# Re-ordering the opening of a transform-then-expert-layer kernel: merged row loads, rows and weight columns on another DMA queue

## The chip, the cores and the metric

The kernel runs on one core of one Trainium2 chip. The metric is the device time of one execution, in microseconds (us). Lower is better. A difference counts as "same" when it is within 2%.

## The reference

```python
def reference(x, moe_w_in, moe_w_out):          # x: 8 x 3008 x 256, float32
    X = np.fft.fft(np.fft.fft(x, axis=1), axis=2).real   # along the rows, then the channels
    h = X.reshape(8 * 3008, 256) @ moe_w_in              # 256 x 2048
    g = h * np.cos(h)
    return g @ moe_w_out                                 # 2048 x 256
```

## The kernel before

The transform along the rows is done with matrices of cosines and sines (`MC`, "the DFT"), and the transform along the channels is multiplied into the weights (`Wc`, `Ws`). Symmetries of the transform let the kernel fold the rows of a batch four to one before it multiplies. After an opening, it repeats one step of about 4.75 us 376 times (DFT work of the next batch comes in between). In a step TensorE (PE) multiplies (`H`, then `pA` to `pD`), ScalarE (ACT) and VectorE (DVE) compute h·cos h, and GpSimd (POOL) makes four sums of blocks (`G<-G`) which TensorE needs. During the steps POOL also folds the rows of the next batch.

All that the change touches happens in the first 120 us. The parts are these.

*Rows of a batch.* Four tiles `xl0` to `xl3` hold one batch. `xl0` and `xl3` are read in row order by direct DMAs, `xl1` and `xl2` against it by gathers on POOL's queue. The last 512 columns of `xl0` and `xl3` come in two halves of 64 partitions.

```python
def spin(**kw):                      # a load on SP's queue, kept in program order
    pin(nc.sync.dma_start(**kw))

def load_x(b, gather=True):
    ...                              # the four gathers, on POOL's queue
    for j, row in ((0, 0), (3, HALF)):
        spin(out=L[j][:, 0 : 4 * ND], in_=xrows(b, row, 4, 128, 4))       # 512 KB
        for h in range(2):                                                # 2 x 128 KB
            spin(
                out=L[j][64 * h : 64 * h + 64, 4 * ND :],
                in_=xrows(b, row + 512 + 2 * h, 4, 64, 2),
            )
```

*Channel 128.* This channel has no mirror image and is treated apart, for all eight batches at once. It is read element by element: four loads of 8 x 768 elements of 4 bytes each ("single-channel loads"), written to a scratch area in DRAM, and read back in another shape as `xs`. POOL folds `xs` in `fold_ext`, which TensorE needs near step 12.

```python
copy(0, 0, 768, 0, 1)                # rows forward and backward, from both ends:
copy(1, 1, 768, SEQ - 1, -1)         # 6144 descriptors of 4 bytes each
copy(2, 0, 768, HALF, -1)
copy(3, 0, 768, HALF, 1)
```

*Weight columns of channel 128.* `fold_sin(q)` computes a quarter of `Ws`, and four small DMAs turn its last row into columns (`wex`).

```python
def fold_sin(q, tag="H"):
    ps = fold_mms(q, 128, tag)
    act(Ws[:, q * 512 : (q + 1) * 512], ps)
    eng = nc.gpsimd if q > 1 else nc.scalar
    for f in range(4):
        c = q * 512 + f * 128
        pin(eng.dma_start(out=wex[q][:, f : f + 1], in_=Ws[127:128, c : c + 128]))
```

*The order of work.* A list of events `at(time, function)`, sorted by a nominal time (T is one step), sets each engine's order. Two entries matter here: the load of batch 1 and POOL's sums of output weights (`sum_weights(i)`, four small operations each, written to `WT`).

```python
for i in range(8):
    at((i - 1) * T + 1.3, lambda i=i: sum_weights(i))
...
l0 = s0 - (8 if b > 1 else 1.5)                          # s0 = 0 for batch 1
at(l0 * T + 0.1, lambda b=b: state.update(L=load_x(b, b == 1)))
```

## Time and profile before

| quantity | value |
|---|---|
| three runs before the prediction | 1984.85, 1979.04, 1977.92 us |
| the profiled execution | 1985.11 us (span of the core 1983.3) |
| TensorE busy | 1941.3 us, 98% |
| share of TensorE in the chain of waits | 92% |

The page of the kernel before begins as follows. The first line is the span, the second gives busy time, share of the span and number of instructions of each engine, the third is the chain that ended last, by engine.

```profile
span 1983.3 us, 28191 instructions
PE 1941.3 (98%) x8863; PEld 1654.7 (83%) x8863; DVE 1416.7 (71%) x2349; ACT 1452.6 (73%) x2791; POOL 1351.8 (68%) x1862
...
PE 92%; DVE 3%; ACT 1%; issue 1%; POOL 1%; DMA 0%; SPq 0%; DVEq 0%; POOLq 0%
```

TensorE is the limit, and the change takes no work from it. Only the 42 us in which it is not busy, and time in which it runs slowly, can be won. The waits of the first 165 us say where they are. The columns are total us, number of waits and the longest one.

```profile
PE pB L265 <- POOL G L274: 23.4, 3, 20.9
...
POOL e L349 <- DMA xl<-in_x_dram: 21.8, 1, 21.8
...
PE pA L265 <- issue: 2.4, 1, 2.4
```

One wait of 20.9 us stands out, and another engine, POOL, waits 21.8 us for rows. The timeline of TensorE in the kernel before shows when. The columns are start, duration, engine, line, operation, tiles and shapes, and in brackets the idle time before it and what ended it.

```profile
22.59 4.40 PE L265 MATMUL H<-w,CC 128*128 128x512 f32 x6 [1.78 <-DMA w<-in_moe_w_in_dram]
26.82 1.45 PE L265 MATMUL pA<-MC,e 128*128 128x189 f32 x8
...
36.40 1.03 PE L265 MATMUL H<-Rr,Wc 128*128 128x256 f32 x4
...
84.03 0.59 PE L265 MATMUL pB<-G,w 128*128 128x256 f32 x2
105.49 1.22 PE L265 MATMUL pB<-G,WT 128*128 128x256 f32 x2 [20.87 <-POOL G L274]
106.51 1.91 PE L265 MATMUL H<-Ir,Ws 127*128 127x256 f32 x4
...
113.10 0.59 PE L265 MATMUL pB<-G,WT 128*128 128x256 f32 x2
```

The first DFT starts at 26.82, step 0 at 36.40 (its first product is `H<-Rr,Wc`). In program order TensorE runs `H` two steps ahead of the products `pA` to `pD`. The first `pA` to `pD`, those of step 0, therefore come after the `H` of step 2, and what is called a wait in step 0 below lies between the starts of steps 2 and 3. From about 84.6 to 105.5 TensorE stands still. The same pair of matmuls takes 1.22 us after the gap and 0.59 us later: it runs at half speed for a while. The timeline of POOL in the kernel before, with the same columns, shows what it waited for.

```profile
76.40 3.02 POOL L274 TENSOR_TENSOR G<-G 128x256 f32<-128x256 f32 x4
101.19 0.20 POOL L349 COPY e<-xl 128x6 f32<-128x6 f32 x1 [21.77 <-DMA xl<-in_x_dram]
101.34 1.93 POOL L328 TENSOR_TENSOR e<-xl 128x381 f32<-128x381 f32 x2
103.24 3.00 POOL L274 TENSOR_TENSOR G<-G 128x256 f32<-128x256 f32 x4
...
129.23 0.40 POOL L274 TENSOR_TENSOR xs<-xs 128x96 f32<-128x96 f32 x1
```

The kernel pins POOL's work in program order (`pin`). Its fold of batch 1 (`e<-xl`) comes before its sums of the next step (`G<-G`), and its rows were late. The timeline of SP's queue in the kernel before tells why; the duration is the time that SP needed to issue a group.

```profile
12.75 5.71 SPq L207 DMA_DIRECT2D w<-in_moe_w_in_dram  x2
...
29.62 48.86 SPq L168 DMA_DIRECT2D x<-in_x_dram  x5
78.60 17.27 SPq L168 DMA_DIRECT2D xl<-in_x_dram  x6
95.91 4.88 SPq L168 DMA_DIRECT2D xe_dr<-x  x4
```

SP's loads are pinned in program order too, and it spent 48.86 us on issuing the single-channel loads (`x<-in_x_dram`, four long ones and a short one) before it could issue batch 1's rows at 78.60. From the completion records in the trace, the four long loads landed at 56.9, 69.4, 83.7 and 98.2 us. That is 12.5 to 14.5 us each.

The windows view of the kernel before gives a stretch and its length, then the busy time (and number of instructions) of PE, PEld (TensorE's weight loads), DVE, ACT and POOL, and then TensorE's mean granted clock, the DMA share and GB/s.

```profile
106.00:112.00 6.00, 6.00 (x17) 4.80 (x16) 1.98 (x3) 1.09 (x2) 5.09 (x8) 0.58 0.58 13
112.00:125.00 13.00, 13.00 (x61) 11.09 (x60) 10.19 (x17) 10.14 (x20) 8.08 (x12) 1.00 0.03 3
```

The half speed is thus the granted clock: 0.58 just after the gap, 1.00 later.

### The profile page before, as it was taken

The numbers are of one execution on the slowest core, as the hardware profiler recorded it, in microseconds if no ns is written. First come the engines' busy times: TensorE is split into PE (matmuls) and PEld (weight loads), VectorE is DVE, ScalarE is ACT, GpSimd is POOL, SyncE is SP. The second block draws the span as 40 slices with busy tenths as digits, with TensorE's granted clock in tenths as the row PEclk, the third lists the DMA queues.
The fourth block names the chain that finished last, engine by engine and source line by source line (L and its number), as shares of the span: only waits on it lengthen the run. The fifth ranks groups of instructions, "written<-read, shape, count | busy, mean of one in ns | idle before, by whom it ended". The sixth has DMA issues, their size and how long they took to land.

```text
span 1983.3 us, 28191 instructions
## 1 busy us (share of the span) xinstructions
PE 1941.3 (98%) x8863; PEld 1654.7 (83%) x8863; DVE 1416.7 (71%) x2349; ACT 1452.6 (73%) x2791; POOL 1351.8 (68%) x1862
## 2 busy tenths in 40 slices
PE   8689999999999999999999999999999999999998
PEld 4568888888888888888888888888888888887887
DVE  4557767777677776777767776777777776677777
ACT  2557777777777777777777777777777777777776
POOL 3578767777587766777667776678667776555664
PEclk9889999999999999999999999999999999999999
DMA  9920220102200021000310003001030110000101
GB/s 264 23 35 20 51 48 15 26 11 53 49 11 20 12 60 45 18 12 14 73 36 12 15 12 85 16 20 25 8 84 11 22 20 15 16 11 12 22 11 23
DMA packets 261506, 66.17 MB, mean 33 GB/s; under 512 B 248499, under 2 KB 251323, under 8 KB 261356
## 3 DMA queue, kind: packets, MB, share of 16 engines
q1 hardware_dynamic: 254188, 51.51, 14.9%
q0 software_dynamic: 3840, 12.59, 2.0%
q8 instruction: 71, 1.16, 0.3%
q14 instruction: 79, 0.65, 0.1%
q10 hardware_dynamic: 3328, 0.27, 0.1%
HBM read 39.48 MB, written 24.79 MB: 32 GB/s over the span
## 4 chain that ended last, share of the span: by engine, by line
PE 92%; DVE 3%; ACT 1%; issue 1%; POOL 1%; DMA 0%; SPq 0%; DVEq 0%; POOLq 0%
PE H L265 36%; PE pB L265 16%; PE pC L265 16%; PE pD L265 16%; PE pA L265 8%; DVE G L719 1%; ACT G L277 1%; DVE v L271 0%; POOL G L274 0%; DMA xl<-in_x_dram 0%; SPq L168 0%; DVE G L271 0%; ACT E L277 0%; DVE M L271 0%; DVE u L271 0%
## 5 line engine op out<-in xcount | busy, mean ns | idle before, releaser
L274 POOL TENSOR_TENSOR G<-G 128x256 f32<-128x256 f32 x1500 | 1076.8, 728 | 565.3 <-DVE G L719 474.1
L719 DVE SCALAR_TENSOR_TENSOR G<-H,G 128x512 f32<-128x512 f32 x376 | 256.9, 683 | 270.4 <-ACT G L277 270.2
L271 DVE TENSOR_TENSOR G<-H,G 128x512 f32<-128x512 f32 x376 | 260.0, 691 | 220.6 <-ACT G L277 217.6
L277 ACT ACTIVATE G<-H 128x512 int32<-128x512 f32 x376 | 224.5, 597 | 256.6 <-DVE G L271 255.2
L265 PE MATMUL pC<-G,WT 128*128 128x256 f32 x1504 | 388.1, 380 | 1.7 <-DVE u L271 1.6
L265 PE MATMUL H<-Ir,Ws 127*128 127x256 f32 x1504 | 388.5, 380 | 0.7 <-ACT E L277 0.7
L265 PE MATMUL H<-Rr,Wc 128*128 128x256 f32 x1504 | 387.1, 380 | 0.8 <-ACT H L277 0.8
L277 ACT ACTIVATE H<-Rb,wex 128x256 f32<-128x256 f32 x752 | 360.1, 479 | 26.1 <-DVE G L719 10.4
L277 ACT ACTIVATE E<-H 128x512 f32<-128x512 f32 x376 | 224.2, 596 | 204.8 <-PE H L265 201.0
L265 PEld LDWEIGHTS H<-Rr,Wc 128*128 128x128 f32 x1504 | 283.7, 190 | 48.6 <-ACT H L277 2.8
L265 PEld LDWEIGHTS pC<-G,WT 128*128 128x128 f32 x1504 | 284.5, 190 | 45.5 <-PE H L265 5.1
L265 PEld LDWEIGHTS H<-Ir,Ws 127*128 127x128 f32 x1504 | 283.0, 190 | 45.3 <-ACT E L277 6.2
L271 DVE TENSOR_TENSOR G<-E,H 128x512 f32<-128x512 f32 x376 | 255.2, 679 | 26.1 <-PE H L265 24.6
L277 ACT ACTIVATE G<-G,halfpi 128x512 f32<-128x512 f32 x376 | 269.5, 717 | 1.5 <-DVE G L271 1.5
L271 DVE TENSOR_TENSOR M<-G,M 128x512 f32<-128x512 f32 x376 | 257.6, 685 | 0.0
L719 DVE SCALAR_TENSOR_TENSOR G<-G,M 128x512 f32<-128x512 f32 x376 | 254.2, 676 | 0.4 <-ACT M L277 0.3
L265 PE MATMUL pB<-G,WT 128*128 128x256 f32 x752 | 227.7, 384 | 23.4 <-POOL G L274 23.4
L277 ACT ACTIVATE M<-M,halfpi 128x512 f32<-128x512 f32 x376 | 246.2, 655 | 0.4 <-DVE M L271 0.3
L265 PE MATMUL pA<-G,w 128*128 128x256 f32 x752 | 223.7, 379 | 2.4 <-issue 2.4
L277 ACT ACTIVATE M<-G 128x512 int32<-128x512 f32 x376 | 224.4, 597 | 0.0
L265 PE MATMUL pD<-G,WT 128*128 128x256 f32 x752 | 224.1, 380 | 0.0
L265 PE MATMUL pD<-G,w 128*128 128x256 f32 x752 | 223.8, 379 | 0.0
(132 smaller groups left out, 1793.4 us busy)
## 6 DMA issues: line engine op xcount, KB each, us to landing
out_dram<-ot SPq DMA_DIRECT2D x496, 32.0 KB
xl<-in_x_dram SPq DMA_DIRECT2D x16, 512.0 KB
xl<-in_x_dram SPq DMA_DIRECT2D x32, 128.0 KB
out_dram<-ot SPq DMA_DIRECT2D x256, 2.0 KB
MC<-dft_mats SPq DMA_DIRECT2D x4, 943.5 KB
Rb<-r SPq DMA_DIRECT2D x10, 376.0 KB
w<-in_moe_w_in_dram SPq DMA_DIRECT2D x4, 512.0 KB
w<-in_moe_w_out_dram SPq DMA_DIRECT2D x1, 2048.0 KB
```

Source lines behind the costliest of these rows:

```text
L265: nc.tensor.matmul(out_, lhsT=lhsT, rhs=rhs, start=start, stop=stop, skip_group_check=True)
L271: pin(nc.vector.tensor_tensor(out=o, in0=a, in1=b, op=op))
L274: pin(nc.gpsimd.tensor_tensor(out=o, in0=a, in1=b, op=op))
L277: pin(nc.scalar.activation(out=o, in_=i, func=func, **kw))
L719: nc.vector.scalar_tensor_tensor(out=o, in0=h, scalar=TWO_PI, in1=c, op0=ALU.mult, op1=ALU.mult)
```

## The change

The intent is to open with fewer transfers, to bring the input weights earlier, and to take batch 1's rows off SP's queue. The core of the diff:

```diff
+        eng = nc.gpsimd if b == 1 else nc.sync
         for j, row in ((0, 0), (3, HALF)):
-            spin(out=L[j][:, 0 : 4 * ND], in_=xrows(b, row, 4, 128, 4))
-            for h in range(2):
-                spin(
-                    out=L[j][64 * h : 64 * h + 64, 4 * ND :],
-                    in_=xrows(b, row + 512 + 2 * h, 4, 64, 2),
+            pin(eng.dma_start(out=L[j][:, 0 : 4 * ND], in_=xrows(b, row, 4, 128, 4)))
+            pin(
+                eng.dma_start(
+                    out=L[j][:, 4 * ND :],
+                    in_=bass.AP(
+                        tensor=xt,
+                        offset=x.offset + (b * SEQ + row + 512) * ND,
+                        ap=[[2 * ND, 2], [4 * ND, 64], [1, 2 * ND]],
+                    ),
                 )
+            )
 ...                                   # loads of CC, w_in, MC, w_out, pick: dma_start -> spin
-        eng = nc.gpsimd if q > 1 else nc.scalar
         for f in range(4):
-            pin(eng.dma_start(out=wex[q][:, f : f + 1], in_=Ws[127:128, c : c + 128]))
+            pin(nc.gpsimd.dma_start(out=wex[q][:, f : f + 1], in_=Ws[127:128, c : c + 128]))
 ...
-    warm(8)
+    warm(3)
 ...
-        (T + 3.2, lambda: I_odd.second("pA")),
+        (T + 3.2, lambda: I_odd.second("pC")),
 ...
-    at(e0 + 3 * T + 1.35, lambda: ext_rows(0, gtt))
+    at(e0 + 5 * T + 1.0, lambda: ext_rows(0, vtt))
 ...
-        l0 = s0 - (8 if b > 1 else 1.5)
+        l0 = s0 - (8 if b > 1 else 0.5)
```

In the smaller lines, `warm(n)` issues n matmuls on zeros, `I_odd.second` is one part of a DFT, which moves from bank pA to pC, and `ext_rows(0)` are small sums for channel 128, which move from POOL (`gtt`) to VectorE (`vtt`). `spin` in place of `dma_start` fixes the place of a load in SP's order.

The second half of `w_in` already stood ahead of the DFT matrices on SP in the kernel before. What can move it in time is that fewer transfers stand ahead of it and that ScalarE's column copies no longer share SP's completion semaphores (in the trace of the kernel before they used six of SP's eight).

The merged transfer covers the 128 partitions in two blocks of 64 with a source whose outermost dimension has size 2.

## The prediction

> **What bounds it now.** TensorE is busy 1941 of 1983 us (page, part 1) and the chain of waits is 92% TensorE, so past about 160 us only TensorE work would help, and the change removes none there. What can be won lies before that.
>
> Three losses, all in the opening:
> 1. *Batch 1's rows.* In the timeline TensorE stops from about 84.6 to 105.5 us (20.9 us, waiting for POOL's sums). POOL stands behind the fold of batch 1, which waited 21.8 us for its rows. They sat on the SP queue behind four single-channel loads of 4-byte elements (24,576 descriptors, about 13.5 us each, landing at 56.9, 69.4, 83.7, 98.2 us), and could be issued only at 78.6 to 95.9. After the stop, matmuls run at half rate for 6 us, costing 3.0 more. Together 23.9 us.
> 2. *Start.* TensorE's DFTs begin at 26.8 us. The second half of w_in lands at 22.5, because SP issued it at 12.75 and 18.13: SP and ACT share eight completion semaphores, and SP waited for older transfers and for ACT's small weight-column copies. Rows for the other fold (xl3) land at 17.6.
> 3. TensorE waits 2.35 us at 52.7 for bank pA; the move of I_odd to pC removes that.
>
> **What the change does.** Batch 1 leaves SP: its rows go on POOL's queue after the gathers, by about 50 us, needed near 80 to 85. I expect loss 1 removed completely. The program's order shows ten opening transfers issued without a wait, which alone would be worth about 5 us.
>
> But the merged transfer has a source whose slowest dimension is 2. The Trainium skill, page "DMA: Bandwidth & Descriptors", section "Why a DMA increments its semaphore by 16 and not by 1", says a DMA is spread over the largest k up to 16 dividing both sides' slowest dimensions: here 2 engines in place of 16. This trace agrees for other sizes: 128-row loads leave 16 completion records, 8-row loads 9 (8 and the sequencer's one), 31-row stores 2. A 2-engine merge puts 64 descriptors of 2 KB (108 ns median) on each of two engines, twice; everything behind them on the ring waits for those two. Estimate from these durations: xl0 complete near 19 us (now 12.9), xl3 near 27 (17.6), w_in near 29 (22.5), w_out near 40 (36.5). The start becomes later by about 5 us, not earlier.
>
> **New wait.** POOL's fold_ext needs the single-channel data (loads end, then a DRAM round trip). It ran at 129.2 and had its data at 113. It would now run near 105 to 110[...]: data near 105 (16 engines) to 115 us (2). POOL and then TensorE wait some 2 to 4 us there. Moving ext_rows(0) to DVE gives back 1 to 2 us (TensorE waited 0.6 and 1.9 us at 145 and 152).
>
> **Sum.** -23.9, +5 (start), +2.5 (fold_ext), -1.5: about -18 (1961 us) with two engines; about -27 (1952) if merged transfers spread over 16. I lean to the first: **1959 us**, range **1946 to 1970**. Faster by over 2%: 0.03; within: 0.96; slower: 0.01.
>
> **Right if** in the timeline the gap near 85 to 105 is gone; the merged loads leave 2 or 3 completion records and xl0/xl3 become ready after 17/24 us; DFTs begin after 30; POOL waits for the xs data before fold_ext. **Wrong if** the merged loads leave 16 records, DFTs begin near 22 and the gain is 25 or more; or if batch 1's rows on POOL's queue starve or hold up POOL's own column copies (they wait for the gathers' landing) so that the sums of step 0 come late.

## More of the kernel before

The kernel before varies by itself. In the three sessions with experiments (seven runs each; every session used one chip, and the three used different ones) it took 1972.6 to 1982.2, 1973.1 to 1988.1 and 1973.4 to 1987.0 us.

## The result

| | before | after |
|---|---|---|
| runs, us | 1984.85, 1979.04, 1977.92, 1979.32 | 1973.09, 1973.71, 1973.28, 1977.32 |
| median, us | 1979.18 | 1973.49 |
| ratio (95% interval) | | 0.997 (0.9947 to 0.9993) |

Ratios here and below are the mean time of one kernel's fast runs over that of the other's fast runs of the same rounds, so they are not quite the ratio of the medians quoted. The change gains 5.7 us by the medians, not 20, and lies outside the predicted range of 1946 to 1970. A repetition in another session gave 1973.36 (see `after_again`).

The page of the kernel after:

```profile
span 1971.3 us, 28169 instructions
PE 1940.8 (98%) x8858; PEld 1654.1 (84%) x8858; DVE 1418.2 (72%) x2354; ACT 1452.6 (74%) x2791; POOL 1355.8 (69%) x1869
...
PE 91%; DVE 3%; DMA 2%; ACT 1%; SPq 1%; issue 1%; POOL 1%; DVEq 0%; POOLq 0%
```

TensorE's work is the same, and DMA has appeared in the chain with 2%. The timeline of TensorE in the kernel after:

```profile
28.71 6.01 PE L271 MATMUL H<-w,CC 128*128 128x512 f32 x8 [10.93 <-DMA w<-in_moe_w_in_dram]
34.55 1.45 PE L271 MATMUL pA<-MC,e 128*128 128x189 f32 x8
...
44.13 1.03 PE L271 MATMUL H<-Rr,Wc 128*128 128x256 f32 x4
...
60.65 0.59 PE L271 MATMUL pB<-G,w 128*128 128x256 f32 x2
65.28 1.22 PE L271 MATMUL pB<-G,WT 128*128 128x256 f32 x2 [4.03 <-POOL G L280]
66.29 1.91 PE L271 MATMUL H<-Ir,Ws 127*128 127x256 f32 x4
...
72.92 0.59 PE L271 MATMUL pB<-G,WT 128*128 128x256 f32 x2
```

The gap between 85 and 105 is gone. In its place TensorE waits 10.93 us for the input weights at the start, the DFT begins at 34.55 instead of 26.82, and step 0 at 44.13 instead of 36.40. Then, in the first products of step 0, there is a new wait of 4.03 us for POOL's sums, followed by matmuls at half speed. The windows view of the kernel after, with the same columns as before, shows the granted clock around it:

```profile
65.00:68.00 3.00, 2.72 (x7) 2.19 (x8) 0.00 (x0) 0.00 (x0) 2.84 (x7) 0.50 0.32 56
68.00:71.00 3.00, 3.00 (x9) 2.37 (x8) 1.98 (x3) 1.09 (x2) 2.84 (x5) 0.51 0.21 1
71.00:74.00 3.00, 3.00 (x15) 2.64 (x14) 0.50 (x1) 1.74 (x4) 1.45 (x4) 1.00 0.55 3
```

The clock is 0.50 for about 6 us. The stretch from 65.28 to the next step's `H<-Rr,Wc` at 71.20 took 5.9 us; at full clock the same stretch takes 3.0 (in `contig_paired` below, from 60.02 to 63.04). So the wait costs 4.0 and the clock another 2.9.

Why the start is late is told by the completion records of the row loads. Each record is one increment of the load's semaphore.

```
load of batch 0                 before: records, last   after: records, last
xl0, first 4 rows (128 rows)    16, 10.05               16, 10.74
xl0, remainder                  16 + 16, 12.73           3, 19.36
xl3, first 4 rows (128 rows)    16, 15.38               16, 20.46
xl3, remainder                  16 + 16, 17.56           3, 27.60
w_in, second half               landed 22.54            landed 29.79
w_out                           landed 36.51            landed 40.37
```

The Trainium skill, page "DMA: Bandwidth & Descriptors", section "Why a DMA increments its semaphore by 16 and not by 1", says that a DMA from SP runs on the largest number of engines up to 16 that divides the slowest dimension of both sides, and that each of these engines posts one increment while the sequencer posts the rest at once. The trace agrees: three records are two engines and the sequencer. The loads behind the merged ones show the two late engines as well: of the 16 records of `w_in`'s last load, 14 came by 21.77 us and the last two at 28.87 and 29.79; of `w_out`'s, 14 came by 33.92 and the last two at 39.48 and 40.37. The same merged form on POOL's queue left 16 records, which agrees with what that section says of transfers issued by GpSimd; there the number of records does not tell how many engines carried the data.

Why POOL's sums of step 0 were late is told by POOL's timeline in the kernel after.

```profile
46.24 1.29 POOL L158 DMA_INDIRECT xl<-in_x_dram,ix  x1 [0.30 <-issue]
...
49.52 0.89 POOL L184 DMA_DIRECT2D xl<-in_x_dram  x1
55.80 0.56 POOL L304 DMA_DIRECT2D wex<-Ws  x1 [5.38 <-ACT vs L283]
...
58.25 1.18 POOL L304 DMA_DIRECT2D wex<-Ws  x2 [0.97 <-DMA xl<-in_x_dram,ix]
59.45 0.47 POOL L280 TENSOR_TENSOR WT<-w 128x128 f32<-128x128 f32 x1
...
63.00 3.02 POOL L280 TENSOR_TENSOR G<-G 128x256 f32<-128x256 f32 x4
...
117.58 0.39 POOL L280 TENSOR_TENSOR xs<-xs 128x96 f32<-128x96 f32 x1
```

The last column copies use completion semaphores that the gathers used just before, so they cannot be issued before the gathers have landed. The gathers landed at 55.24, 56.45, 57.97 and 58.61, and the copies follow at once. The profile puts the first of these waits (5.38 us) down to ScalarE's `vs`, which ended at 55.38, but the copy reads `Ws`, which ScalarE had written by 48.52. What it waited for is taken to be the landing at 55.24; in `unmerged` the profile puts the same wait down to a gather. Behind the copies stand eight sums of output weights (59.45 to 63.0), which step 0 does not need yet, and only then the sums that step 0 needs. The last line is `fold_ext`. Its data had landed at 115.1, so it did not wait here; the margin was 2.5 us.

SP's queue in the kernel after, the same view as before:

```profile
7.25 10.76 SPq L168 DMA_DIRECT2D w<-in_moe_w_in_dram  x2
...
35.39 55.76 SPq L168 DMA_DIRECT2D x<-in_x_dram  x5
91.27 13.82 SPq L168 DMA_DIRECT2D xe_dr<-x  x4
105.14 8.42 SPq L168 DMA_DIRECT2D xs<-xe_dr  x12
```

The second half of `w_in` is issued 5.5 us earlier than before, as intended, yet lands 7 us later. The issue was not what it waited for.

### Where the 12 us between the two profiles come from

Both profiles hold 376 groups `H<-Rr,Wc`, one a step. Their starting times, taken from the two traces, place each gain and loss. The third row is worked out by subtraction.

| start of step, us | 0 | 2 | 3 | 8 | 10 | 14 | 20 | 30 |
|---|---|---|---|---|---|---|---|---|
| before (1985.1 us) | 36.40 | 51.63 | 58.98 | 82.73 | 116.12 | 137.84 | 169.99 | 218.97 |
| after (1973.1 us) | 44.13 | 59.36 | 71.20 | 94.96 | 104.46 | 126.17 | 157.23 | 206.21 |
| difference | +7.7 | +7.7 | +12.2 | +12.2 | -11.7 | -11.7 | -12.8 | -12.8 |

The late start costs 7.7. POOL's lateness in step 0 costs another 4.5 net: 4.0 of wait and 2.9 of clock, less the 2.4 us wait for bank pA that the kernel before had here. The removed gap gives 23.9. A little more is won after step 14. From step 30 on the two kernels run alike.

### The profile page after: what moved, and what is told of

Its sections match the earlier page's. It is cut to its first block, busy times and chain, and to the rows that moved or that the text cites. A ratio compares the mean times of both kernels' runs of the same rounds, so it can differ in the third digit from the quotient of the medians.

```text
span 1971.3 us, 28169 instructions
## 1 busy us (share of the span) xinstructions
PE 1940.8 (98%) x8858; PEld 1654.1 (84%) x8858; DVE 1418.2 (72%) x2354; ACT 1452.6 (74%) x2791; POOL 1355.8 (69%) x1869
## 3 DMA queue, kind: packets, MB, share of 16 engines
HBM read 39.48 MB, written 24.79 MB: 33 GB/s over the span
## 4 chain that ended last, share of the span: by engine, by line
PE 91%; DVE 3%; DMA 2%; ACT 1%; SPq 1%; issue 1%; POOL 1%; DVEq 0%; POOLq 0%
PE H L271 36%; PE pC L271 16%; PE pB L271 16%; PE pD L271 16%; PE pA L271 8%; DMA w<-in_moe_w_out_dram 1%; DVE G L724 1%; ACT G L283 1%; SPq L168 1%; DMA xl<-in_x_dram,ix 1%; DVE v L277 0%; DVE G L277 0%; POOL G L280 0%; DVE M L277 0%; ACT E L283 0%
## 5 line engine op out<-in xcount | busy, mean ns | idle before, releaser
L283 ACT ACTIVATE H<-Rb,wex 128x256 f32<-128x256 f32 x752 | 360.0, 479 | 25.9 <-DVE G L724 10.7
L271 PE MATMUL pB<-G,w 128*128 128x256 f32 x752 | 223.7, 379 | 0.1
```

The lines of the kernel that those rows point to most:

```text
L271: nc.tensor.matmul(out_, lhsT=lhsT, rhs=rhs, start=start, stop=stop, skip_group_check=True)
L283: pin(nc.scalar.activation(out=o, in_=i, func=func, **kw))
```

## The experiments

Three explanations were on the table for the missing gain. They are not exclusive, so the question was how much each explains.

1. The merge: two engines instead of 16 delay the start, and everything else on the same queue.
2. POOL: the copies wait for the gathers' landing and the sums stand in a bad order. If so, sums in another order would give back the loss of step 0.
3. The base: the gap of 20.9 us is not what a typical execution of the kernel before has. The profiled execution, at 1985.1, was 6 us above the median.

Medians are of four runs each. The session's runs of the kernel before stand beside them.

### First session (before: median 1978.54, 1972.59 to 1982.22)

**before_again**: the kernel before, unchanged, for a second profile.

> The kernel before, unchanged, once more. Theory 'baseline': the profile of before came from an execution of 1985.1 us, 6 us over the median of 1979, and its gap at 84.6 to 105.5 us was longer than usual, because the single-channel loads ran slower than in most executions. It expects another profile to show a gap nearer 15 us when its execution is nearer 1979 us, with everything else equal, and a ratio of 1.000. Rival: the gap is always 21 us and the 6 us lie elsewhere; then a 1979 us execution still has a gap of 21 us.

Measured: 1978.71 (1973.90 to 1986.28), ratio 1.0022 (0.9988 to 1.0057). The profiled execution was a quick one, 1973.9. In its timeline of TensorE:

```profile
94.92 1.22 PE L265 MATMUL pB<-G,WT 128*128 128x256 f32 x2 [9.68 <-POOL G L274]
```

The gap is 9.68 us here, not 20.87. From step 8 to step 10 this execution took 21.5 us and the other 33.4; the difference of 11.9 is nearly all of the 11.2 us between the two executions. The four single-channel loads landed at 53.4, 65.2, 77.2 and 88.1 us, 10.9 to 12.0 us apart instead of 12.5 to 14.5. In these two profiles the gap thus follows the speed of these loads, which varies from execution to execution. Why it varies is not settled by any run here. Explanation 3 holds: a profile of an execution 6 us above the median was taken for the typical one.

**unmerged**: the change, with the row loads on SP's queue in two halves again (batch 1's loads on POOL's queue stay merged).

```diff
-                pin(eng.dma_start(out=L[j][:, 4 * ND :], in_=<source [2][64][512]>))   # shortened
+                if b == 1: <as in the change>
+                else:
+                    for h in range(2):
+                        pin(eng.dma_start(out=L[j][64 * h : 64 * h + 64, 4 * ND :],
+                                          in_=xrows(b, row + 512 + 2 * h, 4, 64, 2)))
```

> The changed kernel, but the two merged transfers on the SP queue are two 64-row halves again (batch 1's on POOL stay merged). Theory 'two engines': the halves leave 16 completion records each, xl0 is ready near 12.5 us in place of 19.4, xl3 near 16 in place of 27.6, w_in's second half near 19 in place of 28.6, w_out near 33 in place of 40.4, the DFTs begin near 24 in place of 34.5. Since POOL's chain for step 0 hangs on w_out, the whole gains about 7 us: near 1966. Rival 'bandwidth': the late start is from more bytes being in flight at once; then undoing the merge moves these times by less than 2 us and the whole by less than 2.

Measured: 1962.38 (1959.34 to 1967.50), ratio 0.993 (0.9902 to 0.9959). This is 11.1 us below the changed kernel by the medians. The timeline of TensorE in `unmerged`:

```profile
18.66 5.47 PE L280 MATMUL H<-w,CC 128*128 128x512 f32 x8 [1.16 <-DMA w<-in_moe_w_in_dram]
23.97 1.45 PE L280 MATMUL pA<-MC,e 128*128 128x189 f32 x8
...
33.55 1.02 PE L280 MATMUL H<-Rr,Wc 128*128 128x256 f32 x4
...
53.49 1.22 PE L280 MATMUL pB<-G,WT 128*128 128x256 f32 x2 [2.57 <-POOL G L289]
...
108.44 2.32 PE L280 MATMUL H<-MC,xe 128*8 128x189 f32 x28 [2.30 <-POOL xe L289]
```

With 16 records for each half, the wait for `w_in` shrinks from 10.93 to 1.16 us and step 0 starts at 33.55, which is 10.6 us earlier than with the merge and 2.9 earlier than before. The rest of the intent, fewer waits in the opening, thus works; the merge undid it. A wait of 2.30 us for `fold_ext` appears here: POOL reached it early enough to wait for its data, which landed at 107.39.

**pool_order**: the change, with the weight sums for i = 1 and 2 ahead of the last column copies on POOL (after the transfers of batch 1's rows have been issued).

```diff
-        at((i - 1) * T + 1.3, lambda i=i: sum_weights(i))
+        at(0.9 if i in (1, 2) else (i - 1) * T + 1.3, lambda i=i: sum_weights(i))
```

> The changed kernel, but POOL makes the summed weights of steps 1 and 2 before its last four weight-column copies, which wait for the landing of batch 1's gathers (their semaphores are used again). Theory 'POOL late': the third sum of step 0 is done near 61.7 us in place of 65.2, TensorE's wait of 4.0 us for it and the 3 us of half-rate matmuls after it go nearly away; of these 6.5 us about 2 are lost again because fold_ext then comes before its data (landed at 115): near 1969. Rival: POOL is late because w_out lands late, and its order does not matter: no change.

Measured: 1974.93 (1972.95 to 1975.08), ratio 0.9987 (0.9965 to 1.0010): no gain over the change. The local effect was as expected. The wait in step 0 fell from 4.03 to 1.65 us and the clock stayed at 1.00, so step 3 starts 5.9 us earlier than in the changed kernel (65.33 against 71.20; 1.0 of it was there at step 0 already). But step 14 starts 1.6 us *later* (127.73 against 126.17). The lines between, from the timeline of TensorE in `pool_order`:

```profile
62.20 0.70 PE L271 MATMUL pB<-G,WT 128*128 128x256 f32 x2 [1.65 <-POOL G L280]
...
117.60 4.18 PE L271 MATMUL H<-MC,xe 128*8 128x189 f32 x28 [4.07 <-POOL xe L280]
```

The single-channel data landed at 116.41, at nearly the same time as in the changed kernel (115.11), whatever TensorE did in between. TensorE arrived there earlier and waited 4.07 us, and the 28 small matmuls then took 4.18 us instead of 2.09 (the granted clock from 117.6 to 122 us was 0.50). The loss in step 0 was therefore hidden behind another limit: the chain of single-channel loads. Removing it alone gains nothing. My expectation missed this.

**merge_only**: the kernel before with only the merged form of the row loads.

> The kernel before with one part of the change alone: the merged transfers. Theory 'two engines': DFTs begin near 34.5 us in place of 26.8, w_out lands near 40, the single-channel loads and with them batch 1's rows end 5 to 12 us later, so the gap ends later and the whole loses 8 to 14 us: 1987 to 1993. Rival 'merging helps' (fewer transfers, fewer waits for old semaphores): the DFTs begin at 22 to 25 us and the whole gains or stays.

Measured: 1989.20 (1982.53 to 1994.19), ratio 1.0062 (1.0027 to 1.0097), slower than the kernel before by 10.7 us of the medians. Step 0 starts at 41.96. The gap in the profiled execution is 15.67 us. The merge alone costs what `unmerged` gains by leaving it out.

### Second session (before: median 1980.22, 1973.06 to 1988.11)

**rows_only**: the kernel before with only batch 1's direct rows on POOL's queue (merged there, as in the change); loads on SP in halves.

> The kernel before with one part of the change alone: batch 1's rows go on POOL's queue (merged there, as in the change), everything else as before. Theory 'loss 1': TensorE's gap for batch 1's rows (9.7 to 20.9 us in the two profiles of before, and about 3 us of half-rate matmuls after it) goes away; fold_ext then comes near 105 us, close to the landing of its data, and waits 0 to 3 us: 1961 to 1966. Rival 'moved, not removed': the rows on POOL's queue land late or hold up POOL's own work, and the whole gains less than 5 us.

Measured: 1965.63 (1962.31 to 1967.68), ratio 0.9924 (0.9883 to 0.9964). The gap is gone, the 2.36 us wait for pA is still there, and `fold_ext` now waits for its data (3.8 us on POOL, 3.14 on TensorE). Removing the gap is thus worth 14.6 us net by the medians, not 23.9. The timeline of TensorE in `rows_only`:

```profile
110.95 2.32 PE L280 MATMUL H<-MC,xe 128*8 128x189 f32 x28 [3.14 <-POOL xe L289]
...
132.98 0.73 PE L280 MATMUL pB<-G,WT 128*128 128x256 f32 x2 [1.98 <-POOL G L289]
```

The second wait comes while `ext_rows(0)` is still on POOL, and 3.4 us at half clock follow it. From step 14 to step 20 `rows_only` took 33.9 us, `unmerged` 31.1.

**contig**: the change, but with the rows of the last 512 columns mapped so that one *contiguous* transfer with 128 partitions outermost fills them. Only the DFT constants and the shape of the `xs` loads must follow.

```diff
-    return 4 * p + m if m < 4 else 512 + 4 * (p % 64) + 2 * (p // 64) + m - 4
+    return 4 * p + m if m < 4 else 512 + 2 * p + m - 4
-    low = np.arange(128) < 64
+    low = np.arange(128) % 2 == 0
-                    in_=<source [2][64][512]>,            # shortened
+                    in_=xrows(b, row + 512, 2, 128, 2),
```

> The changed kernel, with rows 512 and up laid on the partitions in order (partition p holds rows 512+2p and 513+2p; the DFT constants are permuted to match), so that the merged transfer is one contiguous 256 KB with 128 rows outermost. Theory 'two engines': it keeps the merge's count of transfers and loses its cost: 16 completion records, DFTs begin near 23 us, and with 8 in place of 12 loads of xs fold_ext's data lands some 2 us earlier than in the unmerged run: 1957 to 1961 against 1962 there. Rival 'merging itself is bad' (transfers in flight): no better than the change, near 1973.

Measured: 1960.32 (1958.28 to 1961.27), ratio 0.9902 (0.9861 to 0.9942). The merged loads leave 16 records and land at 11.87 and 15.60, step 0 starts at 31.68:

```profile
31.68 1.02 PE L267 MATMUL H<-Rr,Wc 128*128 128x256 f32 x4
```

This is a merged transfer that helps: 13 us below the change by the medians. So merging is not at fault, only its outermost dimension of 2.

**order_paired**: the change with `pool_order` and with the four single-channel loads written as two of 16 rows (the shapes of the tiles and of the `xs` loads, which follow from it, are cut here).

```diff
-            copy(0, 0, 768, 0, 1)
-            copy(1, 1, 768, SEQ - 1, -1)
-            copy(2, 0, 768, HALF, -1)
-            copy(3, 0, 768, HALF, 1)
+            copy(rows[0][:, 0:768], 0, 1, HALF, 2 * NB, 768)
+            copy(rows[1][:, 1:768], HALF - 1, -1, HALF, 2 * NB, 767)
```

> pool_order with the single-channel loads changed too: the pairs of rows (row s and half plus s; half minus s and end minus s) are loaded as two 16-row transfers in place of four of 8 rows, so 16 engines take part in place of 8. Theory 'hidden behind': pool_order gained nothing because fold_ext waited 4.7 us for this data (TensorE 4.1 us, and half-rate matmuls after); here the loads leave 16 completion records, end near 75 us in place of 105, fold_ext waits for nothing, and the gain of pool_order appears: 5 to 8 us under it, 1967 to 1970. Rival: the 4-byte loads are bound by the memory and not by the count of engines; they end after 95 us and nothing is gained.

Measured: 1971.71 (1969.94 to 1973.31), ratio 0.9957 (0.9916 to 0.9997), about 2 us more than expected. The paired loads leave 16 records and landed at 78.84 and 91.77: 13 us for twice the rows. `fold_ext` had its data at 101.7 and did not wait. But the wait in step 0 came back (4.41 us, then half clock), because POOL's column copies waited longer for the gathers (3.8, 0.56, 2.61 and 0.38 us). That the paired single-channel loads slowed the gathers is supported by two pairs of runs that differ in the pairing alone, with one profile of each run: the last gather landed at 62.46 us here and at 59.09 in `pool_order`, and at 46.81 in `contig_paired` below and 45.85 in `contig`. By what mechanism is not shown.

**best**: `contig`, `pool_order` and the paired loads together.

> contig, pool_order and the paired single-channel loads together in the changed kernel. If the three account for what the change gave away, no wait over 1 us of TensorE is left between 25 and 160 us: near 1953, range 1950 to 1957. If something else holds it, near 1960.

Measured: 1953.95 (1953.90 to 1955.38), ratio 0.987 (0.9831 to 0.9910), in line with the expectation. Step 0 starts at 31.93, the wait in step 0 is 1.42 us, the `xs` data land at 79.27 and are used at 100.57. This version beats both kernels: by 26 us the one before, and by about 20 us the change.

### Third session (before: median 1976.34, 1973.44 to 1987.03)

**after_again**: the change, unchanged.

> The changed kernel, unchanged, beside the candidates and in the same rounds. Theory: 1973 to 1976, as at first, with a spread of a few us and not the 15 us of the kernel before (whose gap follows the speed of the single-channel loads): fold_ext comes 2 to 3 us after its data's landing. Rival: a spread as wide as before's.

Measured: 1973.36 (1972.57 to 1974.15), ratio 0.998 (0.9942 to 1.0017). The change reproduces within 0.2 us of its first median, while the kernel before moved by 2.8 us between sessions. The gain, 5.7 us at first, is 3.0 here, and the interval of the ratio in the third session does not exclude one.

**contig_paired**: `best` without `pool_order`.

> best without POOL's other order. Theory 'POOL late': the step-0 wait is back, 3 to 5 us and about 2 us of half-rate matmuls after it: 1957 to 1960 against 1954 for best. Rival: once fold_ext's data is early, POOL's order does not matter: 1954.

Measured: 1960.43 (1959.77 to 1961.21), ratio 0.9915 (0.9878 to 0.9952). The wait in step 0 is 4.20 us. So `pool_order`, which gained nothing on the change, is worth 6.5 us here by the medians (`best` is from the second session; against `best_early` in the same session it is 6.0), and `fold_ext` no longer waits for data. This tests the masking seen in `pool_order`, although the setting differs from the change in two parts, the pairing and the row map.

**best_early**: `best` with batch 1's load one step earlier, as in the kernel before.

```diff
-        l0 = s0 - (8 if b > 1 else 0.5)
+        l0 = s0 - (8 if b > 1 else 1.5)
```

> best, and batch 1's load one step earlier, as in the kernel before, so that POOL issues its eight transfers while it waits for w_out, and its copies' wait for the gathers' landing is over when they are due. The last wait of step 0 (1.4 us) goes: 1952 to 1954. If the gathers then compete with w_out and the DFT matrices and delay those, 1954 to 1957.

Measured: 1954.47 (1953.94 to 1955.88), ratio 0.9886 (0.9849 to 0.9923), the same as `best` although TensorE's longest waits from 20 to 160 us fell to about 1 us. Both profiles start the steps after the opening 1.3 us apart (187.89 against 189.21 for step 30), which the medians of the two sessions do not show. I leave this as a tie.

**early_paired**: `best_early`, but with the change's merged loads of outermost dimension 2 (and so with its row map and its twelve `xs` loads). It measures the merge where nothing else hides it.

> The changed kernel with its 2-engine merges kept and all else as in best_early (POOL's order, the early load, paired single-channel loads; original row map). What is left against best_early is the late start alone. Theory: about 11 us later DFTs (33 to 34.5 us against 22 to 23), of which nothing is caught up: 10 to 12 us over best_early, near 1964. Rival: a large part of the late start is absorbed by other waits; under 5 us.

Measured: 1966.45 (1966.08 to 1967.36), ratio 0.9946 (0.9909 to 0.9983). This is 12.0 us above `best_early` in the same session; step 0 starts at 42.94 against 31.67, 11.3 later. TensorE has no other long wait. The whole cost of the merge reaches the end.

### The account

All terms are differences of medians of the sessions.

| step | us | from |
|---|---|---|
| batch 1's rows off SP's queue | -14.6 | `rows_only` against before |
| the rest of the change without the merge | -3.2 | `unmerged` against `rows_only`, different sessions |
| the merge on two engines | +11.1 | change against `unmerged`, different sessions |
| sum | -6.7 | measured -5.7 and -3.0 |

The merge measured in three settings gives 10.7 (`merge_only`), 11.1 and 12.0 us. The terms from different sessions carry an uncertainty of 2 to 4 us, since the kernel before moves by as much.

## Why the prediction was wrong

**What was right.** The gap was removed completely. The merged loads ran on two engines, with 3 records. The single times were near: xl0 predicted near 19 and measured 19.4, xl3 27 and 27.6, `w_in` 29 and 28.6 to 29.8, `w_out` 40 and 40.4, DFT "after 30" and 34.55. It also named, under "wrong if", that the column copies might wait for the gathers' landing and make the sums of step 0 late.

**First failed step: the term "-23.9" for the gap.** The mechanism was right and the size was that of one execution. Between the two profiles the gap did return 23.9 us, but the profiled execution took 1985.1 us and the median is 1979. In a second profile, of a 1973.9 us execution, the gap was 9.7 us. Removed alone, it was worth 14.6 net, including a new 3 us wait for `fold_ext`. The prediction subtracted from the median a loss that it had read from a run 6 us above it. Had it subtracted its other terms from 1985.1, it would at least have been consistent: the changed kernel's profiled execution is 12.0 us below that one, and its time, 1973.1, is its median too.

**Second failed step: "+5 (start)".** The start itself came 7.7 us later, near the step's own times for the loads. But the prediction put it at 5, gave the 2.4 us of bank pA no term of their own (7.7 less 2.4 is 5.3) and left step 0 out of the sum. The sums of step 0 came at 63 to 66 us, TensorE waited 4.0 us for them and then ran 6 us at half clock, which cost another 2.9. By step 3 the change stood 12.2 us behind the kernel before, instead of 5. The risk that was named only as a condition was in fact what happened; with the durations at hand (gathers issued from about 42 us, 10 to 12 us to their landing in the trace of the kernel before, eight sums of 0.46 us) it could have been put into the sum.

**Third failed step: "+2.5 (fold_ext)".** This wait did not occur in the changed kernel, because TensorE and POOL arrived late enough. It occurred in three of the runs that removed one of the other losses: 2.3 us in `unmerged`, 3.1 in `rows_only`, 4.1 in `pool_order`. The term was right as a limit and wrong as an addend. Losses that lie one behind the other in the same chain are partly hidden by each other, and in the change and `pool_order` the single-channel loads set a time near 115 to 116 us before which no other repair helped.

**The last term, "-1.5" for ext_rows(0) on DVE,** was near: between steps 14 and 20 the changed kernel gained 1.1 us on the kernel before.

Added up on the profiled executions: -23.9 (gap) + 12.2 (start and step 0) - 1.1 is -12.8 at step 30, and -12.0 at the end; the prediction's sum was -18. The other 6 us of the miss are the distance of the profiled execution from the median.

**What stays open.** Why the single-channel loads take 10.9 to 12.0 us each in one execution and 12.5 to 14.5 in another is not known; it explains most of the spread of the kernel before. How the paired loads slow the gathers is open too. The separate worth of the move of I_odd to pC, of the column copies on POOL and of ext_rows(0) was not measured by runs: together they and the rest are the -3.2 of the account. The profiles show only that the 2.4 us wait for pA and the 2.8 us of steps 14 to 20 in `rows_only` are gone in `unmerged`.

## What to carry to other kernels

Before merging two transfers, look at the outermost dimension of both sides and, for a load on SP's queue, count the completion records afterwards (on POOL's queue there were 16 here even with an outermost dimension of 2): here one transfer with an outermost dimension of 2 cost 11 us against two halves, and one with 128 partitions outermost was as good as the halves or a little better. Before taking the length of a wait from a profile as what its removal is worth, compare the profiled execution with the median and take a second profile if the kernel varies; then ask which arrival stands next behind that wait, because a repair is worth only the distance to it. A repair that gains nothing alone may be worth its full size (0 became 6.5 us here) once the limit behind it has been moved.

## What the Trainium skill lacked or had wrong

- Page "DMA: Bandwidth & Descriptors", section "Rules for kernel authors": it advises one 128-partition transfer instead of two to disjoint partition halves, and to coalesce small transfers. Here two halves (16 records each) beat the merged transfer (3 records) by 10.7 and 11.1 us of kernel time (`merge_only` against before, the change against `unmerged`). The same section's rule to use all 16 engines does warn of an outermost dimension below 16, but the first rule lacks the condition that the merged transfer must keep a large outermost dimension. With that (`contig`) it holds: 1960.3 against 1962.4 us for the halves, in different sessions, with overlapping intervals of the ratio.
- The same page gives no rule and no figure for the effect of such a transfer on what stands behind it. The next load on the queue, `w_in`, was issued 5.5 us earlier than before and landed 7 us later, with only two of its 16 records late, and the last single-channel load landed at 104.8 us instead of 97.0 (change against `unmerged`).
- The same page has no time for reads of single 4-byte elements. Here 768 of them per engine (by the count of records) took between 8.9 (`best_early`) and 14.5 us (12 to 19 ns each, worked out by division), with a wide spread between executions of one kernel.
- Page "TensorE: Matmul & The Clock Gate", section "What's actually happening": it gives an idle window of about 3.4 us before the clock is halved. In these runs less was enough: a wait of 2.57 us (`unmerged`) and one of 1.98 us (`rows_only`, until 132.98) were each followed by 3.4 us at half clock, one of 4.03 us (the change) by 6 us, and waits of 1.65 (`pool_order`), 2.36 and 3.14 us (`rows_only`) by none of it. So the length of a wait does not decide it, and the place where it falls does. By the clock records of all 14 traces the clock changes only at whole multiples of 3.41 us after the first record. From 40 to 1930 us it fell to half after each of the 12 such stretches in which TensorE was idle for 1.98 us or more, and after none with 1.97 us or less; it came back only after a stretch without idle time, and stayed at half after those with 0.95 us or more. This is worked out from the traces, in which the ends of matmuls are modelled. That the clock is either half or full agrees with the page.
